# Sequence-transform blocks added up by DMAs, and four sums moved into the MLP, in a spectral-mixing GLU kernel on one core

## The chip, the cores and the metric

The kernel runs on one core of a Trainium2 chip. The metric is device time in microseconds (us), the median of several runs. The core's engines are called as in its profile: PE is TensorE (PEld its weight loads), DVE is VectorE, ACT is ScalarE, POOL is GpSimd, SP is SyncE. POOL and SP issue the DMAs here. A DMA that POOL issues can add to what lies at its target (`accum_op=ADD`).

## What the kernel computes

```
xn = layernorm(x)                                   # x: 2048 x 512
a  = xn @ hid_re.T ; b = xn @ hid_im.T              # DFT along the hidden axis, 512
s  = seq_re @ a - seq_im @ b                        # DFT along the sequence, 2048
h  = sigmoid(xn @ w_gate) * (xn @ w_up)             # 512 -> 1792
g  = silu(h @ w_down)                               # 1792 -> 512
out = x + s * g
```

Everything is float32. Each product is made of three matmuls, because each operand is split into a high part (rounded, by ACT, L119) and a low part (the rest, by DVE, L124).

## The kernel before

The work is a list of units, each a handful of matmuls on PE. It is written in three stages, and the order of all instructions is the order in which the program writes them (`manual_schedule`); `sooner(n, f)` and `after(n, f)` put a step ahead of unit n or behind it.

- Sequence transform, units 0 to 111. It is done on xn first (the two DFTs commute). Four chunks t of 512 output columns; every chunk makes seven Strassen-like products k on 2x2 blocks, each in four units (pp) of 12 matmuls. Products 1 and 2 of all chunks come first; then, chunk after chunk, 5, 6, 7, 3, 4. Operands of products 5, 6, 7 and 4 are sums of DFT blocks (t1 to t4). A sum is made on DVE (`onto`, L128) or, as a `Sum`, by a POOL DMA that adds the second block from DRAM onto the page of the first (L232).
- At the end of a product `done(k)` takes its two PSUM banks. `snap` copies them to a page (ACT, L313); `join` subtracts a bank from an earlier snapped page (DVE, L320); `put` sends the page to the DRAM block `f_raw[t][0..3]` (POOL, L308).
- MLP, units 112 to 209: 14 blocks of seven units, each with 12 matmuls of gate and up (PSUM tags ga, ua, gb, ub, gc, uc) and 6 of the down product (tag pd). A finished pd pair is copied out by ACT (L568, L650) or added on DVE (L654) and added to `g_part` in DRAM by a POOL DMA (L559).
- Hidden stage, from unit 210: products of `f_raw` blocks and of their sums `f_sum` with the hidden DFT, times g, onto x. `f_sums(pair, half, at, gap)` makes the four sums that it needs: loads of four `f_raw` blocks (SP, L80), four adds on DVE (L128, 128x1024), four stores (POOL, L746). It is called four times; `w_sums` makes four such sums of the hidden DFT.

All operands live in one pool of 54 pages of 4 KB per partition. A page is given to a new tile when its last reader is done; if this reader is a DMA, the new tile's first writer waits for the landing. POOL's DMAs take the semaphores DMASW0 to DMASW7 in turn, one after another, so a wait on one of them by ACT or DVE can be led back to one DMA of POOL's row.

Of the kernel before, what the change touches and what calls it, by code (L numbers as in the profile page):

```python
# [8 lines left out]
F32 = mybir.dt.float32  # L9
F32R = mybir.dt.float32r  # L10
AF = mybir.ActivationFunctionType
ALU = mybir.AluOpType
ADD, SUB = ALU.add, ALU.subtract
# [9 lines left out]
SB = 512  # L23
# [9 lines left out]
def fnet_glu_kernel(ctx: ExitStack, tc: tile.TileContext, x, x_t, c_re, c_im, w_h, w_gu, w_down, out):  # L33
    nc = tc.nc
# [8 lines left out]
    def page(shape, dtype=F32R):  # L43
        return pages.tile([P, *shape], dtype, name="page")
# [14 lines left out]
    f_raw = [[dram.tile([P, 2, SB], F32, name=f"f_raw{t}{b}") for b in range(4)] for t in range(NT)]  # L59
# [13 lines left out]
    class Load:  # L73
        def __init__(self, src, shape):
            self.src, self.shape, self.at = src, shape, None
# [51 lines left out]
    def combine(dst, a, b, op, engine=None):  # L127
        (engine or nc.vector).tensor_tensor(dst, a, b, op=op)  # L128
        return dst
# [3 lines left out]
    def add(needs, run):  # L133
        units.append((needs, run))
# [3 lines left out]
    def after(n, f):  # L138
        extra.setdefault(n, []).append(f)

    def sooner(n, f):
        early.setdefault(n, []).append(f)
# [95 lines left out]
    def onto(a, b):  # L238

        def make():  # L240
            v = a()
            return combine(v, v, b(), ADD)

        return make


    def c_block(t, pp, j, m):
        v = (c_re, c_im)[m][j, pp, t]
        return Load(halves(v) if pp == j == m == 0 else v, [2, SB])
# [3 lines left out]
    class Chunk:  # L253


        def __init__(self, t, tags):
            self.t, self.tags, self.ps, self.s = t, tags, {}, {}
            self.op, self.total = {}, {}
            for pp in range(4):
                b = {(j, m): c_block(t, pp, j, m) for j in range(2) for m in range(2)}  # L260
                self.op[1, pp] = Parts([b[0, 0]], b[0, 0].load, [2, SB])
                self.op[2, pp] = Parts([b[1, 0]], b[1, 0].load, [2, SB])
                b[0, 0], b[1, 0] = c_block(t, pp, 0, 0), c_block(t, pp, 1, 0)
                b11, b12, b21, b22 = b[0, 0], b[0, 1], b[1, 0], b[1, 1]
                t1 = Value([b11, b12], onto(b11.load, b12.load)) if t else Sum(b11, b12)
                t2 = Value([b22], onto(t1.get, b22.load))
                t3 = Value([b22], onto(b12.load, b22.load)) if t else Sum(b12, b22)
                t4 = Value([b21], onto(t2.get, b21.load))
                for k, v in {5: t1, 6: t2, 7: t3, 4: t4}.items():
                    self.total[k, pp] = v  # L270
                    self.op[k, pp] = Parts([v], v.get, [2, SB])
                self.op[3, pp] = Parts([b22], b22.load, [2, SB])
# [31 lines left out]
            if pp == 3:  # L304
                self.done(k)

        def put(self, block, v):
            nc.gpsimd.dma_start(f_raw[self.t][block], v)  # L308

        def snap(self, name, ch):  # L310
            self.s[name] = page([2, SB], F32)
            for d in range(2):
                nc.scalar.activation(self.s[name][:, d, :], self.ps[ch, d], AF.Copy)  # L313
            return self.s[name]

        def join(self, block, name, ch, swap=False):
            v = self.s[name]
            for d in range(2):
                a, b = v[:, d, :], self.ps[ch, d]
                nc.vector.tensor_tensor(v[:, d, :], *((b, a) if swap else (a, b)), op=SUB)  # L320
            self.put(block, v)

        def done(self, k):
            if k < 3:
                v = self.snap(f"p{k}", "p")
                if k == 2:
                    self.put(0, v)
            elif k == 5:
                self.snap("u5", "c")
            elif k == 6:  # L330
                self.snap("u2", "a")
            elif k == 3:
                self.join(2, "u2", "c")
            elif k == 7:
                self.join(3, "u5", "a", swap=True)
            else:
                self.put(1, self.snap("u4", "a"))

        def add_product(self, k):
            total = (9, 3) if self.t == 0 and k in (5, 7) else (6, 3)  # L340
            for pp in range(4):
                m = len(units)
                if (k, pp) == (6, 0):
                    after(m - 2, self.again)
                if (k, pp) in self.total:
                    sooner(m - total[0], self.total[k, pp].load)
                    sooner(m - total[1], self.total[k, pp].get)
                add(self.needs(k, pp), lambda k=k, pp=pp: self.run(k, pp))
# [156 lines left out]
    def x_norm(h, b, at):  # L505

        c = 2 * h + b
        mean, scale = (v.rearrange("p o -> (p o)").partition_broadcast(P) for v in m_part[c])
        by = Load(scale, [SB])
        raw = [Load(x_t[c * 2 + j], [2, SB]) for j in range(2)]  # L510

        def centre(j):
            nc.gpsimd.dma_start(raw[j].load(), mean.unsqueeze(1).to_broadcast([P, 2, SB]), accum_op=ADD)

        def step(j):
            v = xraw[h, j, b] = raw[j].load()
            nc.vector.tensor_tensor(v, v, by.load().unsqueeze(1).to_broadcast([P, 2, SB]), op=ALU.mult)

        sooner(at[0] - 5, by.load)
        for j in range(2):  # L520
            sooner(at[j] - 9, raw[j].load)
            after(at[j] - 5, lambda j=j: centre(j))
            after(at[j], lambda j=j: step(j))
# [209 lines left out]
    def f_sums(pair, half, at, gap=1):  # L733

        a0, b0 = (Load(f_raw[2 * pair][2 * (half ^ 1) + j], [2, SB]) for j in range(2))
        a1, b1 = (Load(f_raw[2 * pair + 1][2 * (half ^ 1) + j], [2, SB]) for j in range(2))
        t2 = Value([], lambda: page([2, SB], F32))
        steps = (
            (a0.load, a0, a1),
            (a1.load, a1, b1),  # L740
            (t2.get, a0, b1),
            (b0.load, t2, b0),
        )

        def step(i, dst, a, b):
            nc.gpsimd.dma_start(f_sum[pair][half][i], combine(dst(), a.get(), b.get(), ADD))  # L746

        for i, v in zip((0, 0, 1, 3), (a0, a1, b1, b0)):
            sooner(at + gap * i - 3, v.load)
        for i, v in enumerate(steps):  # L750
            after(at + gap * i, lambda i=i, v=v: step(i, *v))
# [158 lines left out]
    with tc.manual_schedule():  # L910
        chunks = begin_seq()
        n = len(units)
        x_norm(0, 0, (n - 30, n - 27))
        x_norm(0, 1, (n - 24, n - 18))
        x_ops(0, (n - 12, n - 10, n - 9, n - 7, n - 6, n - 4, n - 3, n - 2, n - 1, n - 0, n + 2))
        last, job = None, None
        for h, g in BLOCKS:
            made = g == last
            if not made:
                w, wd, last = w_operands(g), Down(g), g  # L920
            job = block(h, w, made, job, Seven(h, wd, made))
        x_norm(1, 0, (n + 10, n + 13))
        x_norm(1, 1, (n + 17, n + 20))
        x_ops(1, (n + 22, n + 24, n + 26, n + 27, n + 28, n + 30, n + 32, n + 33, n + 35, n + 36, n + 38))
        f_sums(0, 0, n - 38, 2)
        f_sums(0, 1, n + 38, 1)
        f_sums(1, 0, n + 54, 1)
        f_sums(1, 1, n + 70, 1)
        w_sums(n + 62)
        for i, (pair, k) in enumerate(itertools.product(range(NT // 2), BLOCK)):  # L930
            if (pair, k) not in ENDS:
                after(n + 2 + 2 * i, lambda pair=pair, k=k: put_x(pair, *BLOCK[k]))
        left = waiting + [(job, k) for k in SEVEN]
        waiting.clear()
        hidden_units(left)
        begin(chunks)
        for n, (needs, run) in enumerate(units):
            for f in early.get(n, []):
                f()
            for k in range(n, min(n + LOAD_AHEAD + 1, len(units))):  # L940
                for p in units[k][0]:
                    p.load()
            ahead = [p for _, (ps, _) in zip(range(SPLIT_AHEAD + 1), units[n:]) for p in ps]
            for p in ahead:
                p.begin()
            for p in ahead:
                p.high()
            for p in ahead:
                p.get()
            for f in middle.get(n, []):  # L950
                f()
            run()
            for f in extra.get(n, []):
                f()
# [62 lines left out]
```

## Time and profile before

| | |
|---|---|
| time, median of 3 runs | 792.49 us (792.35 to 792.52) |
| span of the profiled execution, first to last instruction | 790.8 us |
| PE / PEld / DVE / ACT / POOL busy | 786.3 / 650.8 / 670.1 / 520.9 / 148.6 us |
| bytes moved by DMA | 190.46 MB, mean 241 GB/s |

The profile is of one execution. No time of its own is listed for it apart from its span, which is 1.7 us below the median of the runs. A group of instructions has a line of the kernel, an engine, an operation and out<-in by the program's tile names; then the count, the busy time and the mean duration in ns of one, and the idle time of the engine ahead of them with what ended it. A timeline row has the start and the length in us, the engine, the line, and in brackets the idle time ahead of it and what ended it; equal neighbours are merged (x2). "DMA to landing" is the time from the issue to the completion of a DMA.

### The profile page before, as it was taken

To read this page: it belongs to the slowest core of one execution; us is meant where nothing else is said; L and a number is where in the kernel's file an instruction comes from. 1 tells how busy PE (TensorE), PEld (TensorE's weight loads), DVE (VectorE), ACT (ScalarE), POOL (GpSimd) and SP (SyncE) were. 2 spreads that over 40 slices of the span, in tenths; PEclk is the share of its full clock that TensorE was granted. 3 is DMA by queue.
4 is the path that set the end of the run, shared out by engine and by line. 5 is a ranking of instruction groups with operands and counts; after the bars stand their busy time and mean duration, and the time that the engine had idled before them with its cause. 6 is when DMAs were issued, how large, how long until landed. Compare 5 with 4: busy or idle time off the path is not lost.

```text
span 790.8 us, 9957 instructions
## 1 busy us (share of the span) xinstructions
PE 786.3 (99%) x3466; PEld 650.8 (82%) x3466; DVE 670.1 (85%) x881; ACT 520.9 (66%) x795; POOL 148.6 (19%) x199
## 2 busy tenths in 40 slices
PE   9999999999999999999999999999999999999998
PEld 7888888888888888888888888888888888888886
DVE  6877799978899989899999888668869898896967
ACT  6787575552543555677887767576577787887571
POOL 3525300000021002022111131122222111111301
PEclk9999999999999999999999999999999999999999
DMA  9994988357699446859976996799999898999996
GB/s 345 409 380 124 312 241 278 120 197 279 256 274 361 160 163 224 227 165 229 201 128 96 228 228 186 220 207 294 286 299 265 186 226 219 237 285 316 268 348 169
DMA packets 56306, 190.46 MB, mean 241 GB/s; under 512 B 6208, under 2 KB 6720, under 8 KB 56256
## 3 DMA queue, kind: packets, MB, share of 16 engines
q0 software_dynamic: 23360, 77.62, 45.5%
q1 hardware_dynamic: 32896, 112.21, 38.9%
q8 instruction: 27, 0.44, 0.2%
q14 instruction: 23, 0.19, 0.1%
HBM read 122.68 MB, written 70.27 MB: 244 GB/s over the span
## 4 chain that ended last, share of the span: by engine, by line
PE 99%; DVE 0%; issue 0%
PE pd L71 30%; PE ga L71 15%; PE ua L71 15%; PE uc L71 10%; PE gc L71 10%; PE gb L71 9%; PE ub L71 9%; PE pd L417 0%; PE gb L417 0%; PE ub L417 0%; DVE page L883 0%; DVE page L884 0%
## 5 line engine op out<-in xcount | busy, mean ns | idle before, releaser
L124 DVE TENSOR_TENSOR page<-page 128x512 fp32r<-128x512 f32 (+1 forms) x378 | 343.1, 938 | 69.8 <-ACT page L119 68.5
L119 ACT ACTIVATE page<-page 128x512 fp32r<-128x512 f32 (+1 forms) x378 | 297.2, 829 | 108.0 <-DVE page L128 95.5
L71 PE MATMUL pd<-page 128*128 128x512 f32 x1068 | 259.5, 388 | 0.0
L71 PEld LDWEIGHTS pd<-page 128*128 128x128 f32 x1068 | 199.8, 188 | 41.2
L128 DVE TENSOR_TENSOR page<-page 128x1024 f32<-128x1024 f32 (+2 forms) x244 | 195.4, 820 | 1.2 <-DMA page<-in_w_gu_dram 0.3
L71 PE MATMUL ga<-page 128*128 128x512 f32 x528 | 139.1, 390 | 0.0
L71 PE MATMUL ua<-page 128*128 128x512 f32 x528 | 138.8, 389 | 0.0
L71 PEld LDWEIGHTS ga<-page 128*128 128x128 f32 x528 | 99.3, 188 | 21.4 <-ACT page L363 0.7
L71 PEld LDWEIGHTS ua<-page 128*128 128x128 f32 x528 | 99.4, 188 | 20.6
L559 POOL DMA_DIRECT2D g_part<-page x76 | 66.2, 871 | 265.4 <-ACT page L568 159.9
L568 ACT ACTIVATE page<-pd 128x512 f32<-128x512 f32 x140 | 82.4, 598 | 24.7 <-PE pd L71 17.4
L71 PE MATMUL gc<-page 128*128 128x512 f32 x336 | 88.3, 389 | 0.0
L71 PE MATMUL uc<-page 128*128 128x512 f32 x336 | 88.3, 389 | 0.0
L71 PE MATMUL gb<-page 128*128 128x512 f32 (+1 forms) x336 | 86.8, 385 | 0.0
L71 PE MATMUL ub<-page 128*128 128x512 f32 x324 | 85.3, 389 | 0.0
L71 PEld LDWEIGHTS uc<-page 128*128 128x128 f32 x336 | 63.1, 188 | 13.1
L71 PEld LDWEIGHTS gc<-page 128*128 128x128 f32 x336 | 63.1, 188 | 13.1
L71 PEld LDWEIGHTS gb<-page 128*128 128x128 f32 x336 | 62.2, 188 | 12.6
L71 PEld LDWEIGHTS ub<-page 128*128 128x128 f32 x324 | 60.8, 188 | 12.6
L308 POOL DMA_DIRECT2D f_raw<-page x16 | 9.0, 564 | 190.2 <-DVE page L320 137.5
L676 ACT ACTIVATE page<-ga 128x512 f32<-128x512 f32 x28 | 16.6, 593 | 17.4 <-PE ga L71 13.3
L694 DVE TENSOR_TENSOR page<-page 128x512 f32<-128x512 f32 x28 | 19.3, 689 | 10.0 <-ACT page L691 9.3
(105 smaller groups left out, 392.5 us busy)
## 6 DMA issues: line engine op xcount, KB each, us to landing
g_part<-page POOLq DMA_DIRECT2D x84, 512.0 KB, 7.4
page<-in_c_re_dram SPq DMA_DIRECT2D x60, 512.0 KB, 7.5
page<-in_c_im_dram SPq DMA_DIRECT2D x32, 512.0 KB, 6.2
page<-f_raw SPq DMA_DIRECT2D x28, 512.0 KB, 7.4
page<-in_w_gu_dram SPq DMA_DIRECT2D x22, 512.0 KB, 6.5
f_raw<-page POOLq DMA_DIRECT2D x16, 512.0 KB, 5.8
f_sum<-page POOLq DMA_DIRECT2D x16, 512.0 KB, 7.3
page<-f_sum SPq DMA_DIRECT2D x16, 512.0 KB, 9.9
```

The costliest lines, as they stand in the source:

```text
L71: nc.tensor.matmul(ps, ws[w], ms[m], start=first and i == 0, stop=last and i == 2, skip_group_check=go_on)
L119: nc.scalar.activation(self.parts[0], self.raw, AF.Copy)
L124: nc.vector.tensor_tensor(lo, self.raw, hi.bitcast(F32), op=SUB)
L128: (engine or nc.vector).tensor_tensor(dst, a, b, op=op)
L308: nc.gpsimd.dma_start(f_raw[self.t][block], v)
L559: nc.gpsimd.dma_start(g_part[i], pg, accum_op=ADD)
L568: nc.scalar.activation(pg[:, o, :], po, AF.Copy, scale=float(sign))
L676: nc.scalar.activation(s[k][:, m, :], ps[c + "a"], AF.Copy)
L694: nc.vector.tensor_mul(s[k][:, 0, :], s[k][:, 0, :], ps["u" + tag] if tag else s[k][:, 1, :])
```

## The change

Three things are edited.

```diff
-                t3 = Value([b22], onto(b12.load, b22.load)) if t else Sum(b12, b22)
+                t3 = Value([b22], onto(b12.load, b22.load)) if t % 2 == 0 < t else Sum(b12, b22)
...
-        def put(self, block, v):
-            nc.gpsimd.dma_start(f_raw[self.t][block], v)
-
-        def snap(self, name, ch):
-            self.s[name] = page([2, SB], F32)
+        def put(self, block, v, onto=False):
+            nc.gpsimd.dma_start(f_raw[self.t][block], v, **({"accum_op": ADD} if onto else {}))
+
+        def snap(self, ch, sign=1):
+            v = page([2, SB], F32)
             for d in range(2):
-                nc.scalar.activation(self.s[name][:, d, :], self.ps[ch, d], AF.Copy)
-            return self.s[name]
-
-        def join(self, block, name, ch, swap=False):
-            v = self.s[name]
-            for d in range(2):
-                a, b = v[:, d, :], self.ps[ch, d]
-                nc.vector.tensor_tensor(v[:, d, :], *((b, a) if swap else (a, b)), op=SUB)
-            self.put(block, v)
+                nc.scalar.activation(v[:, d, :], self.ps[ch, d], AF.Copy, scale=float(sign))
+            return v
 
         def done(self, k):
...
-            elif k == 5:
-                self.snap("u5", "c")
-            elif k == 6:
-                self.snap("u2", "a")
-            elif k == 3:
-                self.join(2, "u2", "c")
-            elif k == 7:
-                self.join(3, "u5", "a", swap=True)
             else:
-                self.put(1, self.snap("u4", "a"))
+                block, ch, sign, onto = {5: (3, "c", -1, False), 6: (2, "a", 1, False), 7: (3, "a", 1, True), 3: (2, "c", -1, True), 4: (1, "a", 1, False)}[k]
+                self.put(block, self.snap(ch, sign), onto)
 
         def add_product(self, k):
-            total = (9, 3) if self.t == 0 and k in (5, 7) else (6, 3)
+            total = (9, 3) if isinstance(self.total.get((k, 0)), Sum) else (6, 3)
...
-        f_sums(0, 0, n - 38, 2)
         f_sums(0, 1, n + 38, 1)
+        f_sums(0, 0, n + 58, 1)
         f_sums(1, 0, n + 54, 1)
         f_sums(1, 1, n + 70, 1)
         w_sums(n + 62)
```

- Per chunk, blocks 2 and 3 of `f_raw` are no longer joined on DVE. All five products are snapped by ACT, two of them with the sign turned, and the second page of each block is added to the first in DRAM by an accumulating put.
- The sum t3 of chunks 1 and 3 is made by a POOL DMA; chunk 0 had that already, chunk 2 keeps the DVE sum.
- The four sums `f_sums(0, 0)` go from behind units 74 to 80 (every second one; n is 112) to behind units 170 to 173. They stand now between `f_sums(1, 0)` (166 to 169) and `w_sums` (174 to 177).

In sum DVE has 24 instructions less (16 joins, 8 sums), ACT 16 more, POOL 16 DMAs more (8 puts, 8 sums), SP as many as before.

The rows of each engine show what that does around unit 166 to 173. First POOL's row, from the put of a down product that stands ahead of `f_sums(1, 0)`. Behind each row stand the semaphores that it waits for. Before:

```order
L559 DMA g_part5_89<-page_4582 128x1024 [waits DMASW7_49,Activation_49]
L746 DMA f_sum100_116<-page_4454 128x1024 [waits DVE_49]
L559 DMA g_part7_91<-page_4619 128x1024 [waits DMASW4_49,Activation_49]
L746 DMA f_sum101_117<-page_4456 128x1024 [waits DVE_49]
L559 DMA g_part6_90<-page_4661 128x1024 [waits DMASW3_49,Activation_49]
L746 DMA f_sum102_118<-page_4665 128x1024 [waits DMASW2_49,DVE_49]
L746 DMA f_sum103_119<-page_4556 128x1024 [waits DVE_49]
L559 DMA g_part0_84<-page_4699 128x1024 [waits DVE_49]
L559 DMA g_part2_86<-page_4775 128x1024 [waits DMASW5_49,Activation_49]
```

And now:

```order
L545 DMA g_part5_89<-page_4581 128x1024 [waits DMASW3_49,Activation_49]
L732 DMA f_sum100_116<-page_4453 128x1024 [waits DVE_49]
L545 DMA g_part7_91<-page_4622 128x1024 [waits DMASW0_49,Activation_49]
L732 DMA f_sum101_117<-page_4455 128x1024 [waits DVE_49]
L545 DMA g_part6_90<-page_4666 128x1024 [waits DMASW7_49,Activation_49]
L732 DMA f_sum102_118<-page_4670 128x1024 [waits DMASW6_49,DVE_49]
L732 DMA f_sum103_119<-page_4555 128x1024 [waits DVE_49]
L545 DMA g_part0_84<-page_4704 128x1024 [waits DVE_49]
L732 DMA f_sum000_108<-page_4590 128x1024 [waits DMASW1_49,DVE_49]
L545 DMA g_part2_86<-page_4784 128x1024 [waits DMASW2_49,Activation_49]
L732 DMA f_sum001_109<-page_4592 128x1024 [waits DMASW3_49,DVE_49]
```

The puts up to `g_part0` are the same ones in the same order; the new stores `f_sum00x` stand between the later ones. Their semaphores go round in turn: before, `g_part5` has DMASW5, then 6, 7, 0, and the put of `g_part6` DMASW1; now `g_part5` has DMASW1, then 2 and 3, `f_sum101` DMASW4 and the put of `g_part6` DMASW5.

Second, ACT's row at the same place. L568 and L650 (now L554 and L636) take pd banks, L119 makes high parts, L682 (now L668) seeds gb and ub. Before:

```order
L691 ACTIVATE page_4509<-page_4509 128x512 [waits DVE_49]
L119 ACTIVATE page_4631<-page_4458 128x512 [waits DMASW4_49,Activation_49]
L119 ACTIVATE page_4633<-page_4489 128x512
L682 ACTIVATE gb_4651<-ga_4637 128x512 [waits PE_49]
L682 ACTIVATE ub_4653<-ua_4644 128x512 [waits PE_49]
L568 ACTIVATE page_4661<-pd_4611 128x512 [waits PE_49]
L568 ACTIVATE page_4661<-pd_4612 128x512 [waits PE_49]
L119 ACTIVATE page_4671<-page_4522 128x512 [waits DVE_49]
L119 ACTIVATE page_4673<-page_4539 128x512 [waits DVE_49]
L650 ACTIVATE page_4699<-pd_4691 128x512 [waits DMASW7_49,PE_49,Activation_49]
L650 ACTIVATE page_4699<-pd_4692 128x512 [waits PE_49]
L119 ACTIVATE page_4709<-page_4669 128x512 [waits DVE_49]
```

And now:

```order
L677 ACTIVATE page_4508<-page_4508 128x512 [waits DVE_49]
L119 ACTIVATE page_4636<-page_4457 128x512 [waits DMASW1_49,Activation_49]
L119 ACTIVATE page_4638<-page_4488 128x512
L668 ACTIVATE gb_4656<-ga_4642 128x512 [waits PE_49]
L668 ACTIVATE ub_4658<-ua_4649 128x512 [waits PE_49]
L554 ACTIVATE page_4666<-pd_4614 128x512 [waits PE_49]
L554 ACTIVATE page_4666<-pd_4615 128x512 [waits PE_49]
L119 ACTIVATE page_4676<-page_4521 128x512 [waits DVE_49]
L119 ACTIVATE page_4678<-page_4538 128x512 [waits DMASW4_49,DVE_49]
L636 ACTIVATE page_4704<-pd_4696 128x512 [waits PE_49]
L636 ACTIVATE page_4704<-pd_4697 128x512 [waits PE_49]
L119 ACTIVATE page_4716<-page_4674 128x512 [waits DMASW5_49,DVE_49,Activation_49]
```

The instructions are the same. What moved are the pages: four of them now hold `f_raw` blocks, so the new tiles get pages that were freed later. The second row waited for DMASW4 (the `g_part7` put ahead of `g_part5`) and waits now for the put of `g_part5`; the ninth now waits for the store `f_sum101`; the last one now waits for the put of `g_part6`, whose page is written in the sixth and seventh row.

Third, DVE's row somewhat later, from the high parts of the last rows above to L654 (now L640), which adds a pd pair. Before:

```order
L124 TENSOR_TENSOR page_4709<-page_4669,page_4709 128x512 [waits PE_49,Activation_49]
L124 TENSOR_TENSOR page_4711<-page_4509,page_4711 128x512 [waits DMASW6_49,Activation_49]
L128 TENSOR_TENSOR page_4586<-page_4539,page_4586 128x512
L654 TENSOR_TENSOR page_4699<-page_4699,pd_4728 128x512 [waits DMASW7_49,PE_49]
L654 TENSOR_TENSOR page_4699<-page_4699,pd_4729 128x512 [waits PE_49]
L128 TENSOR_TENSOR page_4669<-page_4458,page_4522 128x512
```

And now:

```order
L124 TENSOR_TENSOR page_4716<-page_4674,page_4716 128x512 [waits DMASW5_49,Activation_49]
L124 TENSOR_TENSOR page_4718<-page_4508,page_4718 128x512 [waits PE_49,Activation_49]
L128 TENSOR_TENSOR page_4585<-page_4538,page_4585 128x512
L640 TENSOR_TENSOR page_4704<-page_4704,pd_4735 128x512 [waits PE_49]
L640 TENSOR_TENSOR page_4704<-page_4704,pd_4736 128x512 [waits PE_49]
L128 TENSOR_TENSOR page_4590<-page_4590,page_4592 128x1024 [waits DMAHW7_49,DMAHW6_49]
L128 TENSOR_TENSOR page_4674<-page_4457,page_4521 128x512
```

The first of them has the same new wait, for the put of `g_part6`. The first moved sum (128x1024) stands right behind L640.

More of the change, by code (lines that the diff above doesn't have):

```diff
@@ L305, in run @@
                 self.done(k)
-        def put(self, block, v):
-            nc.gpsimd.dma_start(f_raw[self.t][block], v)
-        def snap(self, name, ch):
-            self.s[name] = page([2, SB], F32)
+        def put(self, block, v, onto=False):
+            nc.gpsimd.dma_start(f_raw[self.t][block], v, **({"accum_op": ADD} if onto else {}))
+        def snap(self, ch, sign=1):
+            v = page([2, SB], F32)
             for d in range(2):
-                nc.scalar.activation(self.s[name][:, d, :], self.ps[ch, d], AF.Copy)
-            return self.s[name]
-        def join(self, block, name, ch, swap=False):
-            v = self.s[name]
-            for d in range(2):
-                a, b = v[:, d, :], self.ps[ch, d]
-                nc.vector.tensor_tensor(v[:, d, :], *((b, a) if swap else (a, b)), op=SUB)
-            self.put(block, v)
+                nc.scalar.activation(v[:, d, :], self.ps[ch, d], AF.Copy, scale=float(sign))
+            return v
         def done(self, k):
             if k < 3:
-                v = self.snap(f"p{k}", "p")
+                v = self.s[f"p{k}"] = self.snap("p")
                 if k == 2:
                     self.put(0, v)
-            elif k == 5:
-                self.snap("u5", "c")
-            elif k == 6:
-                self.snap("u2", "a")
-            elif k == 3:
-                self.join(2, "u2", "c")
-            elif k == 7:
-                self.join(3, "u5", "a", swap=True)
-            else:
-                self.put(1, self.snap("u4", "a"))
+            else:
+                block, ch, sign, onto = {5: (3, "c", -1, False), 6: (2, "a", 1, False), 7: (3, "a", 1, True), 3: (2, "c", -1, True), 4: (1, "a", 1, False)}[k]
+                self.put(block, self.snap(ch, sign), onto)
         def add_product(self, k):
-            total = (9, 3) if self.t == 0 and k in (5, 7) else (6, 3)
+            total = (9, 3) if isinstance(self.total.get((k, 0)), Sum) else (6, 3)
             for pp in range(4):
```

## The prediction

> **What bounds the kernel now.** I read the page first: the span, the busy times, the clock and the chain that ended last.
>
> ```profile
> span 790.8 us, 9957 instructions
> PE 786.3 (99%) x3466; PEld 650.8 (82%) x3466; DVE 670.1 (85%) x881; ACT 520.9 (66%) x795; POOL 148.6 (19%) x199
> PEclk9999999999999999999999999999999999999999
> PE 99%; DVE 0%; issue 0%
> ```
>
> The chain is PE alone, at full clock. The view by stages shows whether a stage has room:
>
> ```profile
> 100.00:310.00 210.00, 210.00 (x928) 173.87 (x927) 191.91 (x186) 106.01 (x127) 14.02 (x20) 1.00 0.69 232
> 520.00:560.00 40.00, 40.00 (x178) 33.10 (x178) 33.03 (x51) 28.77 (x51) 10.25 (x14) 1.00 1.02 257
> ```
>
> PE is busy for 210 of 210 us in the sequence transform and 40 of 40 at the place to which the four sums go. Six matmuls follow each other every 1.36 us there (below), 227 ns each. So nothing taken from DVE can make the kernel shorter; only PE's idle time at both ends, 790.8 - 786.3 = 4.5 us, is to be had, and the change touches neither end. The question is only whether PE has to wait somewhere. [...]
>
> The sum is made against this execution: 790.8 us of span and 1.7 us around it give the median of 792.49.
>
> **Part 1: joins become snaps and accumulating puts.**
>
> ```profile
> L320 DVE TENSOR_TENSOR page<-pd,page 128x512 f32<-128x512 f32 x4 | 2.8, 690 | 4.6 <-PE pd L71 4.6
> L313 ACT ACTIVATE page<-pd 128x512 f32<-128x512 f32 x12 | 7.0, 602 | 11.6 <-PE pd L71 11.6
> ```
>
> DVE loses 16 x 0.69 = 11 us, ACT gets 16 x 0.60 = 9.6 us. In 100 to 310 us ACT is busy for 106 of 210, so this fits. Each new snap makes ACT wait for the end of a product; behind it in ACT's row stands the next high part. The products that are snapped already do the same with PE at 210 of 210. The second put of a block must wait for the landing of the first, which stands eight units (eight times two of the 1.36 us, 21.8 us) ahead. Price on PE: 0; the cover is ACT's idle half.
>
> **Part 2: t3 of chunks 1 and 3 by DMA.** Eight sums of 128x1024 leave DVE, eight accumulating DMAs come to POOL. Chunk 0's eight are the rows to read:
>
> ```profile
> L232 POOL DMA_DIRECT2D page<-in_c_im_dram x8: 875/1097/1956, 71.4 to 100.9; - x8
> DMA to landing us min/median/max: 8.5/11.6/20.3
> ```
>
> They are issued nine units, 24 us, ahead of their use, and wait on POOL for at most one snap (a unit or two). 11.6 us fit, 20.3 us just. Price 0, up to 2 us if all land last.
>
> **Part 3: the four sums between unit 170 and 173.** DVE gets 4 x 1.2 us there and loses them around 210 us, where nobody waits for them. But DVE's time is not what counts first. The sums hold four more pages, from the loads (ahead of unit 167) to the landing of the stores, and ACT's row now waits for puts that were issued just ahead. The rows of ACT, POOL, DVE and PE there:
>
> ```profile
> 529.86 1.14 ACT L119 ACTIVATE page<-page 128x512 fp32r<-128x512 f32 x2
> 530.91 0.58 ACT L682 ACTIVATE gb<-ga 128x512 f32<-128x512 f32 x1
> 532.03 1.28 ACT L568 ACTIVATE page<-pd 128x512 f32<-128x512 f32 x2
> 537.86 0.64 ACT L119 ACTIVATE page<-page 128x512 fp32r<-128x512 f32 x1
> ...
> 525.74 0.86 POOL L559 DMA_DIRECT2D g_part<-page  x1 [3.52 <-ACT page L691]
> 533.60 0.85 POOL L559 DMA_DIRECT2D g_part<-page  x1 [1.72 <-ACT page L568]
> ...
> 539.36 1.47 DVE L124 TENSOR_TENSOR page<-page 128x512 fp32r<-128x512 f32 x2
> 541.35 1.28 DVE L654 TENSOR_TENSOR page<-page,pd 128x512 f32<-128x512 f32 x2
> ...
> 535.23 1.52 PE L71 MATMUL pd<-page 128*128 128x512 f32 x6
> 536.59 1.52 PE L71 MATMUL gb<-page 128*128 128x512 f32 x6
> 543.39 1.52 PE L71 MATMUL pd<-page 128*128 128x512 f32 x6
> ```
>
> Call L the time from the issue of a put to its landing.
>
> - First wait. The `g_part5` put is issued at 525.74. The L119 of 529.86 now needs its page, so it is L - 4.1 us late. Behind it in ACT's row, with no idle time to take it up, stand another L119, two seeds and the copy of the pd banks (532.03). The first bank is free at 532.03 + 0.60 = 532.63, and PE wants it at 535.23: 2.6 us of slack. PE waits for L - 6.7 us.
> - Second wait. The second bank's copy ends L - 4.1 late too, and with it the `g_part6` put of 533.60; this lands at 533.60 + (L - 4.1) + L = 529.5 + 2L. The L119 of 537.86 now needs this page. DVE's L124 of 539.36 needs the same page and that high part, and L654 stands behind it. From the start of this L119 it is 0.64 us to its end and 541.35 + 0.68 - 539.36 = 2.67 to the end of the first L654: 529.5 + 2L + 3.3. PE wants that pd bank at 543.39. So PE stands S = 2L - 10.6 us behind, the first wait included.
>
> The waits between them (the ninth ACT row on `f_sum101`; `f_sum102` and `f_sum103` further on) ask for less by the same reckoning, as their stores are issued from DVE adds that are not late at first. The landings:
>
> ```profile
> L559 POOL DMA_DIRECT2D g_part<-page x6: 847/860/879, 521.4 to 545.8; - x6
> DMA to landing us min/median/max: 5.1/7.7/9.4
> ...
> L559 POOL DMA_DIRECT2D g_part<-page x5: 852/868/879, 543.1 to 558.9; - x5
> DMA to landing us min/median/max: 6.2/8.4/9.4
> ```
>
> These are the puts of 520 to 546 us, then those of 540 to 562. With the fastest of the first, 5.1 us, S is below zero and nothing is lost; with the median S is 4.8, with the slowest 8.2. I take L = 8.3: four loads of 0.5 MB more fall into this stretch, and the later stretch, which moves more bytes, has a median of 8.4. S = 6.0 us. Below zero is excluded, since PE has no idle time there.
>
> [...]
>
> The four adds themselves come behind that. DVE's time there and its next tight step, L654 again:
>
> ```profile
> 541.00:557.00 16.00, 16.00 (x73) 13.23 (x72) 12.54 (x22) 11.55 (x20) 3.48 (x4) 1.00 1.04 297
> ...
> 557.42 1.22 DVE L128 TENSOR_TENSOR page<-page 128x1024 f32<-128x1024 f32 x1
> 568.75 1.37 DVE L654 TENSOR_TENSOR page<-page,pd 128x512 f32<-128x512 f32 x2
> ...
> 571.95 1.52 PE L71 MATMUL pd<-page 128*128 128x512 f32 x6
> ```
>
> 12.5 us of work in 16 become 12.5 + 4 x 1.22 = 17.4: DVE falls 1.4 us back. The first L654 ends at 569.43 and PE wants the bank at 571.95, so 2.5 us of slack take that up. Together with what the second wait leaves behind on DVE (L654 there used up its whole slack of 543.39 - 542.03 = 1.4) it can come to 2.8, some tenths over. Price 0 to 1.5 us, taken as 0.
>
> SP's other loads keep their order there, with four `f_raw` loads among them, so that a load now also waits for the pages of those ahead. The `w_down` load, behind the first two, has the least:
>
> ```profile
> 523.54 0.33 SPq L80 DMA_DIRECT2D page<-in_w_down_dram  x1
> 544.95 0.87 DVE L128 TENSOR_TENSOR page<-page 128x256 f32<-128x256 f32 x2
> ```
>
> It is issued at 523.54 and its page is first read at 544.95. With a landing of 9.4 us as the slowest put above, 12 us are left. Price 0.
>
> The places from which the four sums are taken (loads at 186 to 208 us) become easier on DVE and DMA; PE was not waiting, so that gives nothing.
>
> **Sum.** 792.5 + 0 + 0 + 6.0 + 0 = 798.5 us. A difference under 0.2% (1.6 us) can't be told from no change in this kernel.
>
> **Rivals.**
> - Not slower: the puts land fast enough. S reaches 1.6 us at L = 6.1, so it needs both puts under about 6.1 us. For it: the fastest put took 5.1. Against it: that is 1.6 us below the median of the stretch, with more bytes on the way. [...] An earlier place with ACT waits of the same sort speaks for it, too:
>
> ```profile
> 485.03 0.64 ACT L119 ACTIVATE page<-page 128x512 fp32r<-128x512 f32 x1 [1.93 <-DMA g_part<-page]
> ```
>
>   PE lost nothing there; but that wait is 1.9 us, under the 2.6 of slack, while the first wait here is 8.3 - 4.1 = 4.2. Time 792.5, chance 0.15.
> - Much slower: the waits feed on themselves. A late copy makes a late put, which frees the next page late; a third such turn in the same rows (a put on a page that the next unit needs) would add about L - 4.1 = 4.2 us, and slow loads of the next w_gu pages more. From L = 9.4 on (S = 8.2) and with the 1.5 of DVE it is 802 to 806. For it: four stores of 0.5 MB more follow in 545 to 560. Against it: each wait of PE also gives the DMAs time. Chance 0.13.
> - Faster, since DVE is relieved in the sequence transform: at most the 4.5 us at the ends, of which it reaches none. [...] Chance 0.02.
> - The forecast, 794 to 802: chance 0.70.
>
> **Numbers.** Slower 0.70 + 0.13 = 0.83, same 0.15, faster 0.02. The range goes from L = 5.8 (S = 1.0, 793.5 us) to a third turn in part (804 us); the case of no change lies below it.
>
> **What would show it.** The row of the high parts, and what their engine waits for ahead of them:
>
> ```profile
> L119 ACT ACTIVATE page<-page 128x512 fp32r<-128x512 f32 (+1 forms) x378 | 297.2, 829 | 108.0 <-DVE page L128 95.5 <-DVE page L694 5.5 <-DMA g_part<-page 3.1
> ```
>
> Right: PE idle for about 6 us between 533 and 550 us and gapless elsewhere; a wait of ACT's L119 on `g_part` DMAs that is over 8 us in total there (3.1 us in the whole kernel now); DVE's L124 waiting on `g_part` too; the copies of pd, L554, late by some 4 us; all snaps of the sequence transform on time. Wrong: puts that land in 6 us there, or PE gaps at 160 to 175 or 270 to 285 us (the sums by DMA land late), or behind 557 (DVE).

## The result, and the profile after

The changed kernel takes 803.23 us (median of 4 runs, 801.9 to 803.76) against 792.46 (792.35 to 792.52): slower by a ratio of 1.0133, 95% interval 1.012 to 1.0145, some 10.5 us. The profiled execution is the fastest of the four: 801.9 us, span 800.0, 9.2 us over the span before.

The page of the changed kernel, its head and the chain that ended last:

```profile
span 800.0 us, 10013 instructions
PE 788.0 (99%) x3466; PEld 651.1 (81%) x3466; DVE 651.2 (81%) x857; ACT 528.9 (66%) x811; POOL 164.6 (21%) x215
PE 88%; DMA 6%; issue 4%; POOL 1%; DVE 1%; ACT 0%; SPq 0%; POOLq 0%; ACTq 0%; DVEq 0%
```

DVE has 19 us less work, as the change says, and the kernel is longer. The chain was PE alone; now 6% of it are DMAs. The stages of the changed kernel show where (a row has the stretch and its length, the busy time and instructions of PE, PEld, DVE, ACT and POOL, the granted clock, the DMA share and GB/s):

```profile
100.00:310.00 210.00, 210.00 (x928) 173.88 (x927) 168.84 (x159) 113.88 (x142) 25.42 (x31) 1.00 0.85 251
528.00:544.00 16.00, 14.24 (x62) 11.16 (x61) 11.22 (x16) 6.85 (x13) 3.37 (x5) 1.00 1.02 301
544.00:548.00 4.00, 1.44 (x7) 0.86 (x5) 0.00 (x0) 0.34 (x1) 0.00 (x0) 1.00 1.03 345
548.00:552.00 4.00, 1.13 (x3) 0.93 (x4) 3.67 (x6) 2.73 (x6) 0.28 (x1) 0.84 0.50 202
552.00:556.00 4.00, 4.00 (x15) 3.17 (x14) 3.97 (x8) 3.34 (x7) 2.00 (x3) 0.73 0.76 119
556.00:580.00 24.00, 24.00 (x108) 19.87 (x107) 22.50 (x31) 15.20 (x27) 7.15 (x11) 1.00 1.05 302
```

In the sequence transform PE is busy for 210 of 210 us. All is lost between 528 and 556 us: in 544 to 548 no engine does anything for most of the time, while the DMAs are at 1.03. The granted clock is 0.84 and 0.73 behind the wait. The rows there, of the changed kernel:

```profile
524.98 0.86 POOL L545 DMA_DIRECT2D g_part<-page  x1 [3.04 <-ACT page L554]
533.84 1.15 ACT L119 ACTIVATE page<-page 128x512 fp32r<-128x512 f32 x2 [3.63 <-DMA g_part<-page]
536.52 1.65 PE L71 MATMUL pd<-page 128*128 128x512 f32 x6 [1.59 <-ACT page L554]
537.25 0.85 POOL L545 DMA_DIRECT2D g_part<-page  x1 [5.82 <-ACT page L554]
539.90 0.63 ACT L119 ACTIVATE page<-page 128x512 fp32r<-128x512 f32 x1 [2.42 <-DMA f_sum<-page]
541.07 1.65 PE L71 MATMUL pd<-page 128*128 128x512 f32 x6 [0.17 <-ACT page L636]
547.66 1.15 ACT L119 ACTIVATE page<-page 128x512 fp32r<-128x512 f32 x2 [6.16 <-DMA g_part<-page]
548.33 1.29 DVE L124 TENSOR_TENSOR page<-page 128x512 fp32r<-128x512 f32 x2 [5.33 <-ACT page L119]
550.14 1.28 DVE L640 TENSOR_TENSOR page<-page,pd 128x512 f32<-128x512 f32 x2
550.87 2.93 PE L71 MATMUL pd<-page 128*128 128x512 f32 x6 [5.43 <-DVE page L640]
553.60 1.80 PE L71 MATMUL ga<-page 128*128 128x512 f32 x6
```

These are the predicted steps in their order. The `g_part5` put of 524.98 lands just before L119 starts at 533.84 (8.9 us); the copy of the pd banks is late and PE waits for 1.6 us. The `g_part6` put, issued late at 537.25, releases the next L119 at 547.66 (10.4 us); L124 and L640 follow, and PE waits for 5.4 us. Between them the wait on `f_sum101` reaches PE too, with some tenths. Then PE is slow: six matmuls in 2.93 us in place of 1.52, and 1.80 for the next six. The time lost at the lower clock is 4 x (1 - 0.84) + 4 x (1 - 0.73) = 1.7 us. By the starts of the matmuls, which also count that the first six behind a wait can be slower (1.65 us in place of 1.52 at 536.52), the three waits cost 1.9 + 0.4 + 5.6 = 7.9 us; with 1.7 it is 9.6, and 0.5 came back in the first 7 us, where the first loads vary from run to run.

The other three runs of the changed kernel had a mean clock of 0.996 where the profiled one had 0.998: 0.002 x 800 = 1.6 us more at the lower clock, which is about the difference between 801.9 and the 803.5 of the others. That is by their mean clocks alone; their rows are not on record.

### The profile page after: what moved, and what is told of

Same layout as the page of the kernel before. It is cut to its first block, busy times and chain, and to the rows that moved or that the text cites. A ratio compares the mean times of both kernels' runs of the same rounds, so it can differ in the third digit from the quotient of the medians.

```text
span 800.0 us, 10013 instructions
## 1 busy us (share of the span) xinstructions
PE 788.0 (99%) x3466; PEld 651.1 (81%) x3466; DVE 651.2 (81%) x857; ACT 528.9 (66%) x811; POOL 164.6 (21%) x215
## 4 chain that ended last, share of the span: by engine, by line
PE 88%; DMA 6%; issue 4%; POOL 1%; DVE 1%; ACT 0%; SPq 0%; POOLq 0%; ACTq 0%; DVEq 0%
PE pd L71 27%; PE ga L71 13%; PE ua L71 13%; PE gb L71 9%; PE ub L71 9%; PE gc L71 9%; PE uc L71 9%; DMA g_part<-page 5%; DMA page<-in_c_re_dram 0%; POOL g_part L545 0%; POOL g_part L548 0%; DVE page L640 0%; ACT page L554 0%; DVE page L124 0%; ACT page L119 0%
## 5 line engine op out<-in xcount | busy, mean ns | idle before, releaser
L124 DVE TENSOR_TENSOR page<-page 128x512 fp32r<-128x512 f32 (+1 forms) x378 | 342.9, 940 | 108.7 <-ACT page L119 107.4
L119 ACT ACTIVATE page<-page 128x512 fp32r<-128x512 f32 (+1 forms) x378 | 296.7, 828 | 82.0 <-DVE page L128 50.6
L128 DVE TENSOR_TENSOR page<-page 128x1024 f32<-128x1024 f32 (+2 forms) x236 | 186.2, 808 | 2.6 <-DMA g_part<-page 1.3
L554 ACT ACTIVATE page<-pd 128x512 f32<-128x512 f32 x140 | 82.2, 598 | 25.1 <-PE pd L71 17.4
L308 POOL DMA_DIRECT2D f_raw<-page x24 | 16.4, 681 | 193.1 <-ACT page L313 178.1
L662 ACT ACTIVATE page<-ga 128x512 f32<-128x512 f32 x28 | 16.6, 594 | 16.7 <-PE ga L71 12.6
## 6 DMA issues: line engine op xcount, KB each, us to landing
page<-in_c_im_dram POOLq DMA_DIRECT2D x16, 512.0 KB, 10.6
```

The lines of the kernel that those rows point to most:

```text
L119: nc.scalar.activation(self.parts[0], self.raw, AF.Copy)
L124: nc.vector.tensor_tensor(lo, self.raw, hi.bitcast(F32), op=SUB)
L308: nc.gpsimd.dma_start(f_raw[self.t][block], v, **({"accum_op": ADD} if onto else {}))
L554: nc.scalar.activation(pg[:, o, :], po, AF.Copy, scale=float(sign))
L662: nc.scalar.activation(s[k][:, m, :], ps[c + "a"], AF.Copy)
```

## The experiments

**The parts one by one.** First the changed kernel with the four sums at their old place, that is parts 1 and 2 alone (the diff), and the kernel before with the move alone (the reverse of it).

```diff
-        f_sums(0, 0, n + 58, 1)
+        f_sums(0, 0, n - 38, 2)
```

> The changed kernel with f_sums(0, 0) back at its old place (behind units 74 to 80); the snaps with accumulating puts and the t3 sums by DMA stay. If the whole loss comes from the four moved sums: the time of before, 792.5 within 1 us, PE without a gap over 0.2 us after 10 us. If the DMAs that add up in the sequence transform cost part of it: over 794 us, with PE gaps between 90 and 310 us.

> The kernel before with the four sums f_sums(0, 0) alone moved to behind units 170 to 173. If they are the whole cause: 801 to 804 us as the changed kernel, with two PE gaps (about 2 us at 536, 5 to 6 us at 550) and a lower clock for some 4 us behind them. If the other two parts take a share: under 799 us.

The move alone gives 801.85 us (801.31 to 803.57; ratio 1.0124, 1.0109 to 1.0139): nearly the whole loss, as expected if the sums are its cause. Its waits of PE:

```profile
PE pd L71 <- DVE page L654: 4.7, 1, 4.7
PE pd L71 <- ACT page L568: 1.3, 1, 1.3
```

The same two (the lines of the kernel before are 14 higher). But parts 1 and 2 alone are not free: 796.42 us (795.34 to 799.37; ratio 1.0062, 1.0039 to 1.0086). Two stretches of this kernel (parts 1 and 2 alone):

```profile
200.00:235.00 35.00, 35.00 (x156) 29.00 (x155) 30.58 (x27) 17.37 (x22) 6.35 (x9) 1.00 0.91 295
235.00:270.00 35.00, 34.32 (x150) 27.71 (x149) 27.79 (x24) 16.93 (x21) 8.46 (x10) 1.00 1.06 320
```

The same kernel's waits of DVE at 255 to 280 us, then those of PE at 100 to 310 us (total, times, longest):

```profile
DVE page L128 <- DMA page<-in_c_im_dram: 5.8, 5, 2.5
```
```profile
PE pd L71 <- DVE page L124: 1.4, 2, 0.8
PE gc L71 <- DVE page L124: 0.7, 1, 0.7
```

SP's loads of the DFT blocks come late, DVE's sums (L128) wait for them, and PE for the low parts. The time from issue to landing of these loads at 225 to 280 us, in the kernel before, then in the changed kernel, then with parts 1 and 2 alone (count, KB, median us):

```profile
page<-in_c_im_dram SPq DMA_DIRECT2D x8, 512.0 KB, 15.0
```
```profile
page<-in_c_im_dram SPq DMA_DIRECT2D x8, 512.0 KB, 12.2
```
```profile
page<-in_c_im_dram SPq DMA_DIRECT2D x8, 512.0 KB, 20.4
```

It is the landings that are late more than the issues: the last of the eight is issued at 249.7 us against 248.0 in the changed kernel, and lands at 273.8 against 264.1. So the DMAs of parts 1 and 2 and of the four sums crowd each other at the old place. In the changed kernel the move takes the sums away, the DMA share of 200 to 235 us falls from 0.91 to 0.62, and PE waits for nothing there:

```profile
200.00:235.00 35.00, 35.00 (x156) 29.00 (x155) 25.76 (x23) 17.62 (x23) 4.20 (x5) 1.00 0.62 188
235.00:270.00 35.00, 35.00 (x156) 28.99 (x155) 32.30 (x29) 19.14 (x24) 9.03 (x10) 1.00 1.06 301
```

Is it one of the two parts, or both together? For part 1 alone the line of t3 goes back, in the kernel with parts 1 and 2; for part 2 alone it is changed the other way, in the kernel before (with the line of `total` that goes with it).

```diff
-                t3 = Value([b22], onto(b12.load, b22.load)) if t % 2 == 0 < t else Sum(b12, b22)
+                t3 = Value([b22], onto(b12.load, b22.load)) if t else Sum(b12, b22)
```

> Part 1 alone: the snaps and accumulating puts, with the t3 sums and f_sums(0, 0) as in the kernel before. Eight accumulating puts add 8 MB of reading and writing in DRAM over 160 us. If each part alone fits into the DMAs and only both together with f_sums(0, 0) at the old place crowd them: 792.5 to 793.5 us. If the puts are what makes loads late at 262 to 277 us: 795 us or more, with PE gaps there.

> Part 2 alone: t3 of chunks 1 and 3 by DMA, joins and f_sums(0, 0) as in the kernel before. It moves the same blocks, but loads the first ones nine units ahead in place of six, and the sum goes through the DMAs. If only all together crowd the DMAs: 792.5 to 793.5 us. If the DMA sums are what makes PE wait at 262 to 277 us: 795 us or more, with PE gaps there.

Part 1 alone: 792.86 us (ratio 1.0003, 0.9993 to 1.0012). Part 2 alone: 792.52 us (1.0004, 0.9995 to 1.0013). PE waits there for 0.4 and 0.7 us in their profiles. Each alone fits; both together with the sums cost 4 us. (The page of part 1 alone counts 4.2 MB more written in DRAM than before and no more read; the reading that was in my 8 MB is not in that count.)

**Pages or bytes.** The four moved sums hold pages, and they move 4 MB. Two kernels take one of the two away. First, in the changed kernel, thin sums that hold the same pages from load to store (C is 16):

```diff
+            return v, lambda: nc.sync.dma_start(v.get()[:, :, :C], block[:, :, :C])
...
+            nc.vector.tensor_tensor(p, q, r, op=ADD)
+            nc.gpsimd.dma_start(few[i], p)
```

Second, in the kernel with parts 1 and 2 alone, eight DMAs of 0.5 MB at the new place that hold none:

```diff
+            sooner(at + gap * j - 3, lambda i=i, v=v: nc.sync.dma_start(spare[i], v))
+            after(at + gap * i, lambda i=i, v=v: nc.gpsimd.dma_start(spare[4 + i], v))
```

> The changed kernel with the four moved sums made thin: loads, adds and stores of 16 of the 512 columns, while the pages are held from the same load to the same store; the hidden stage then reads f_raw blocks in place of these four sums. If the pages are the cause: PE still waits at 536 and 550, for S = 2L - 10.6 with the landings L of the two g_part puts; with 6.5 to 8.5 us for L, 795 to 800 us. If the bytes of the sums or their four DVE adds are the cause: 792.5 within 1 us.

> The reverse: f_sums(0, 0) stays at its old place, and at the new place only eight DMAs of 0.5 MB from DRAM to DRAM are issued (four by SP, four by POOL), which hold no page. If the pages are the cause: 792.5 within 1.5 us, although the puts of this stretch land later, 8 to 11 us. If the bytes are the cause: over 796 us, with PE gaps at 536 or 550.

Thin sums: 797.43 us (795.53 to 799.23; ratio 1.0064, 1.004 to 1.0089). Two of the four runs took 795.5 and 795.6 us and two 799.2; only one of the former has a profile. Rows of ACT that waited in it, behind 540 us, with the put that the first of them waits for:

```profile
533.82 0.85 POOL L545 DMA_DIRECT2D g_part<-page  x1 [2.42 <-ACT page L554]
...
540.47 1.15 ACT L119 ACTIVATE page<-page 128x512 fp32r<-128x512 f32 x2 [2.42 <-DMA g_part<-page]
542.81 0.60 ACT L677 ACTIVATE page<-gb 128x512 f32<-128x512 f32 x1 [1.19 <-DMA f_sum<-page]
546.97 0.60 ACT L662 ACTIVATE page<-ga 128x512 f32<-128x512 f32 x1 [2.52 <-DMA f_sum<-page]
```

PE's waits of this kernel behind 300 us, and a window over them:

```profile
PE ga L71 <- ACT page L662: 2.3, 1, 2.3
PE pd L71 <- DVE page L640: 0.6, 1, 0.6
```
```profile
540.00:552.00 12.00, 9.13 (x39) 6.93 (x38) 8.88 (x18) 7.58 (x14) 3.29 (x5) 1.00 1.03 297
```

The rows are the same ones, but the two puts land in 5.4 us (by the landings in the trace) and 6.6 us (540.47 - 533.82), so PE's first wait is gone (ACT still waits for 0.9 us) and 0.6 us of the second remains. Another 2.3 us go behind L662, whose page waits for the store `f_sum103`. The pages alone make PE wait, then; without the bytes the loss is less than half by the median (5.0 of 10.8 us), and 3 to 7 us in single runs.

The bytes alone: 800.93 us (800.59 to 802.17; ratio 1.0112, 1.0097 to 1.0127), 4.5 us over parts 1 and 2 alone, on which it is built. That is not the 792.5 that I gave the page theory, for two reasons. Parts 1 and 2 bring their own 4 us (4.1 us of PE's time at 263 to 277 us in this profile), and the bytes do something too, as ACT's row shows:

```profile
545.07 1.09 ACT L636 ACTIVATE page<-pd 128x512 f32<-128x512 f32 x2 [2.56 <-DMA g_part<-page]
```

The puts of 521 to 538 us take 9.2 to 10.4 us here, and this copy of a pd pair waits for a page freed by the `g_part7` put; the kernel before has this wait as well, where it came to 0.3 us. PE stands for 2.0 us, and the clock falls again (0.78 and 0.79 in 544 to 552 us). These eight DMAs move more in DRAM than the sums do: by the profiles' pages they add 4.2 MB read and 4.2 MB written to parts 1 and 2 alone, while thin sums leave out 2.0 MB of each. Neither pages nor bytes alone are the cause: the page order sets which landing ACT waits for, the bytes set how late it is.

**Other places.** The page order can be read off the program for any place of the four sums. Behind units 122 to 125 and 178 to 181 I read that it stays as before. Behind units 156 to 159 I read that puts issued 3.6 to 4.2 us ahead come to be waited for, much as in the changed kernel. The diff is the first of the three; the others have n + 66 and n + 44.

```diff
-        f_sums(0, 0, n + 58, 1)
+        f_sums(0, 0, n + 10, 1)
```

> The changed kernel with f_sums(0, 0) behind units 122 to 125, at the start of the MLP. There the rows get their pages as in the kernel before: every page that waits for a put was freed by one issued at least 6.8 us ahead. If page waits and crowded DMAs were the whole loss: 792.5 within 1.5 us, no PE gap over 0.5 us behind 10 us, also none at 262 to 277 us. If the sums cost PE time wherever they stand in the MLP (four more DVE adds, 4 MB of traffic): 796 us or more.

> The changed kernel with f_sums(0, 0) eight units later, behind units 178 to 181, next to f_sums(1, 1) and w_sums. The traffic stays in the same crowded stretch (540 to 600 us), but the rows get their pages as in the kernel before. If it takes both the late pages and the bytes: 792.5 to 795 us, with PE gaps of 2 us at most. If the crowded DMAs alone do it: 797 to 802 us.

> The changed kernel with f_sums(0, 0) behind units 156 to 159, right behind f_sums(0, 1). By the page numbers four rows of ACT and DVE at 488 to 495 us then need a page whose put was issued only 3.6 to 4.2 us ahead (3.7 to 4.3 us in the changed kernel at 530 to 543 us). If page waits do it: PE gaps of 4 us or more in total between 480 and 500 us, 796 to 803 us. If the loss belongs to the special traffic at 520 to 560 us: 792.5 to 794 us.

At n + 10: 793.78 us (ratio 1.0017, 1.0008 to 1.0027). At n + 66: 793.73 us (1.0017, 1.0007 to 1.0026), with 1.0 us of waits of PE behind 300 us, and, in a window over the sums and the rows behind them:

```profile
PE ga L71 <- ACT page L662: 1.0, 2, 0.6
```
```profile
540.00:600.00 60.00, 60.00 (x266) 49.71 (x265) 50.93 (x74) 39.37 (x70) 15.87 (x23) 1.00 1.04 316
```

The sums stand eight units later, the DMA share is 1.04 for 60 us, and PE is busy for 60 of 60 (its 1.0 us of waits come at 602 and 607). The puts issued from 561 to 583 us take 12.3 to 17.2 us there, more than anywhere in the changed kernel's stretch, and cost PE no more than that 1.0 us: the rows that waited for a DMA there were ready for the page 10 us or more behind its issue. At n + 44: 800.66 us (798.87 to 801.2; ratio 1.01, 1.0085 to 1.0115). The window of the loss, and the PE rows in it:

```profile
480.00:500.00 20.00, 15.65 (x54) 12.02 (x53) 14.27 (x24) 9.53 (x18) 2.16 (x4) 0.83 0.66 215
```
```profile
484.17 2.40 PE L71 MATMUL pd<-page 128*128 128x512 f32 x6 [1.98 <-ACT page L636]
493.88 1.93 PE L71 MATMUL ga<-page 128*128 128x512 f32 x6 [2.36 <-ACT page L662]
```

All three times came as forecast, but at n + 44 not by the rows that I had named. Those are the ones from 488 us on, where the DMA share is 0.45: the puts and stores issued at 490 to 497 us land in 3.0 to 4.0 us there, and no row waits for them. The rows that wait stand ahead of them: an L119 at 472.45 us (for 3.6 us, on a put issued 4.8 us before ACT was ready for the page), the L636 of 483.52 (3.0 us) and an L119 at 487.04 (1.9 us). Their puts, of 464 to 478 us, take 8.3 to 8.9 us, at a DMA share of 1.00 to 1.07; the kernel before has 1.01 to 1.06 there. PE waits for 4.3 us in sum, and two stretches at a lower clock follow (20 x (1 - 0.83) = 3.4 us lost). So here the place decides by the pages that it takes away, and a short lead cost something only where the landing was slow: 8.3 to 8.9 us, not 3.0 to 4.0.

Whose are the 1.3 us that remain at n + 10?

> The kernel before with f_sums(0, 0) alone moved, to behind units 122 to 125, where the page order stays as it was. If the 1.3 us that the changed kernel still lost with the sums there belong to the sums: 793 to 794 us. If they belong to parts 1 and 2: 792.0 to 792.7 us. Not under 791.5 us by any theory, since PE has no idle time to give.

The kernel before with the sums at n + 10: 793.08 us (ratio 1.0007, 0.9998 to 1.0016). That is at the edge of the first answer, and within the 0.2% that can't be told from no change. The two profiles say more. Behind the first 12 us, PE's matmuls start late at the same two places in both, 368 and 429 us, by 0.9 us in sum in the changed kernel and by 0.6 in the kernel before, and nowhere else up to 770 us. So most of it belongs to the sums; the rest, 0.3 us, is too little to be told. No version was faster than the kernel before.

**The clock.** In the changed kernel 20 matmuls (FILLS) that add zero to a bank fill the long wait, in unit 171 (FILL).

```diff
+            if now[0] == FILL:
+                for _ in range(FILLS):
+                    nc.tensor.matmul(ps[tag], zeros[:, :P], ones, start=False, stop=True, skip_group_check=True)
```

> The changed kernel with 20 matmuls (4.5 us) that add zero to the ua bank, in the 5.6 us in which PE waited ahead of the pd product at 550.87 us. They hold nobody up who isn't late already. If the half clock behind the wait (1.7 us in the profile, one stretch of 3.4 us) comes from PE standing idle: no lower clock at 550 us, and the time is 1.7 us shorter or more, 799 to 801.5 us. If it comes from anything else: 802 to 804 us with the lower clock as before.

801.4 us (800.33 to 801.48; ratio 1.0109, 1.0092 to 1.0126), 1.8 under the changed kernel. Two of the four runs have a mean clock of 1.0, the profiled one among them, and two of 0.998, so some lower clock was left in those. PE's rows (its lines are 2 higher) and two windows:

```profile
546.59 4.53 PE L696 MATMUL ua<-const-float32-1.0,const-float32-0.0 128*128 128x512 f32 x20
551.03 1.66 PE L73 MATMUL pd<-page 128*128 128x512 f32 x6
553.40 1.64 PE L73 MATMUL ga<-page 128*128 128x512 f32 x6 [0.70 <-ACT page L664]
```
```profile
548.00:552.00 4.00, 4.00 (x19) 3.21 (x18) 3.51 (x6) 2.24 (x5) 0.12 (x1) 1.00 0.74 299
552.00:556.00 4.00, 3.30 (x14) 2.39 (x14) 3.97 (x8) 3.62 (x8) 2.15 (x3) 1.00 0.72 120
```

The pd product starts at the same time, takes 1.66 us in place of 2.93, and the clock stays at 1.00. Some of the gain turns into the next wait (L664, 0.7 us), which the slow matmuls had covered. The first wait, which is not filled, is 1.9 us here in place of 1.6; so the profiled spans differ by 0.4 us only (799.6 and 800.0). With the wait filled the half clock behind it is gone (1.00 in place of 0.84 and 0.73): in this kernel PE's standing idle in that wait is what cost the clock.

## Why the prediction was right, and where it was not

- *PE has no time to give; DVE's 19 us are worth nothing.* Right. PE stays the bound, and nothing became faster.
- *Part 1 and part 2 at 0.* Right in the changed kernel (210 of 210 us) and for each alone. But I named ACT's idle half and the nine units of lead as their cover, and did not look at the DMAs as the thing that fills up. Both parts with the sums at the old place cost 4 us: the third part of the change is what covers the first two.
- *"That gives nothing"*, of the place that the sums leave. Right as a term against the kernel before, wrong in its reason, that PE was not waiting there: with parts 1 and 2 PE would wait, and the move gives back those 4 us.
- *First and second wait, S = 2L - 10.6.* The place, the rows, the order and the waiting engines were right; L119 waits on `g_part` DMAs for 9.8 us, where over 8 were forecast. With the measured 8.9 and 10.4 us for the two landings it gives 8.9 + 10.4 - 10.6 = 8.7; 7.9 were lost. The mis-sized term is L: I took 8.3 for both, from the stretch of 540 to 562 us. The four moved sums crowd the DMAs of this very stretch, and with thin sums L was 5.4 and 6.6. I had counted their loads only as a reason to go a little above the median, and had taken one L for both puts.
- *The waits on f_sum101 to f_sum103 "ask for less".* Nearly: 0.4 us on the first in the changed kernel. With thin sums, the one on `f_sum103` was 2.5 us, and PE waited behind it for 2.3: the less the first two waits take, the more this one shows, and the formula for S has no term for it.
- *The clock* was not in the sum. It is 1.7 us in the profiled run, and by the mean clocks about 3.2 in the three others. It was put at nothing without a reason. That and L take the likeliest 798.5 to 803.2: the size was right only within a wide range.
- *Four adds on DVE, 0 to 1.5 us, taken as 0; SP's loads 0.* Right: 24 of 24 us busy behind 556.
- *The rivals.* The time lies outside the "794 to 802" of the forecast and in the interval of "much slower". Of that rival's conditions one came, landings from 9.4 us on (8.9 and 10.4, 9.65 in the mean); the third turn did not: behind 556 us PE waits for nothing. What made up the difference were later landings and the clock.

## What to carry to other kernels

In a pool of pages that is in full use, moving a step moves which landing each later row waits for. Before moving one, list for each wait of ACT and DVE on a DMA how long ahead that DMA was issued, and how long such DMAs take to land there. The shortest lead on which a row waited in the MLP, from the issue of the put to the engine being ready for the page, was 4.2 us in the changed kernel and with the move alone and 4.8 at n + 44, and these lost 8 to 10.5 us. It was 5.8 at n + 10 and 5.9 at n + 66 (not the 6.8 that I had read off the program), and these lost 1.3, though one of them is only eight units away. On an engine without idle time, price a wait with what it does to the clock behind it, too (nothing with thin sums, 1.7 us in the changed kernel, 3.4 with the move alone); and try the parts of a change together as well as alone, as one may be what makes room for another.

## What the runs showed of the hardware

In the changed kernel PE was slow behind its wait of 5.4 us. The mean clocks of 0.84 and 0.73 over two times 4 us come to 3.4 us at half speed, and the trace's record of the clock has 0.50 for 3.41 us from 550.73 us on. The move alone, where the wait is 4.7 us, lost twice as much (4 x 0.42 + 4 x 0.43 = 3.4 us; at the same 0.50 that is 6.8 us):

```profile
549.00:553.00 4.00, 0.74 (x2) 0.65 (x3) 3.29 (x6) 2.60 (x5) 0.00 (x0) 0.58 0.71 291
553.00:557.00 4.00, 4.00 (x12) 3.15 (x11) 3.97 (x7) 3.29 (x7) 2.11 (x3) 0.57 0.68 112
```

The shorter waits of PE, each in the profiled execution of its kernel:

| kernel | wait of PE | granted clock behind it |
|---|---|---|
| changed kernel, first wait | 1.6 us | 1.00 in 536 to 548 us |
| with the 20 matmuls, first wait | 1.9 us | 1.00 in 540 to 560 us, mean of the run 1.0 |
| bytes alone | 2.0 us | 0.78 and 0.79 in 544 to 552 us |
| n + 44 | 2.0 and 2.4 us | 0.83 in 480 to 500 us |
| thin sums | 2.3 us | 1.00 in 544 to 560 us |

The bytes alone lost 4 x 0.22 + 4 x 0.21 = 1.7 us by it, n + 44 twice that, thin sums nothing. So a wait of 2.0 us was followed by a lower clock in these profiles and one of 2.3 us was not: the length of a wait alone does not tell what it costs. What does is not settled by these runs.
